# Batch 0's MLP over five feature steps on both token halves side by side, with a new order of mixing, weight steps and the second batch's scans

## The chip, the cores and the metric

The kernel runs on one core of a Trainium2 chip. The metric is the device time of one execution in microseconds (us). Engines are named as in the profile: PE (TensorE), DVE (VectorE), ACT (ScalarE), POOL (GpSimd) and SP (SyncE, which only issues transfers here).

## What is computed

Three stages follow each other for 4 batches of 768 tokens. A gated linear attention with 8 heads of width 48, whose outputs side by side are a row x of 384:

```
state = alpha[:, :, t, :, None] * state + einsum('bhd,bhe->bhde', k[:, :, t], v[:, :, t])
y[:, :, t] = einsum('bhd,bhde->bhe', q[:, :, t], state)
```

Then a mixer over tokens of rank 32 and an MLP over channels with 1536 features, and last a gating stage:

```
h = x.transpose(0, 2, 1) @ U @ V
u = x + h.transpose(0, 2, 1)
x2 = u + maximum(u @ w_ch1, 0.0) @ w_ch2

h = maximum(x2 @ w_in, 0.0)
u, v = h[..., :512], h[..., 512:]
v_n = (v - mean(v)) / sqrt(var(v) + 1e-06)
out = (u * (einsum('ts,bsd->btd', w_spatial, v_n) + b_spatial[None, :, None])) @ w_out
```

The weights of mixer, MLP and gating arrive as 64-bit words and are turned into float32 on the chip.

## The kernel before

The 768 tokens of a batch are two halves ("blocks") of 384, kept channels first: a block is a tile of 128 partitions x 3 feature tiles m x 384 tokens. Every large product is taken as three matmuls, of the high and low parts of its factors (`mm3`, L238 to L243).

**Scan.** The 8 heads of a batch make four pairs. `prepare` (L606) makes the running products of alpha with two scans on DVE (bw, L613; fw, L625) and scales k and q by them on POOL (L603). A `Pair` then has its transpositions on PE (`flip`, L654, tile ps_kt, copied by ACT to kn), two groups of scores (L669, ps_sc), masks on DVE (L678, sm), a state group (L694, ps_d) that DVE scans to after (L700) and ACT copies to state, and output groups (L716 inner, L725 outer, ps_y) that ACT copies (L738). `attend` (L800 on) yields between these as steps.

**Mixing.** `Mix` transposes a feature tile (L763, ps_t), ACT copies it (L770), PE multiplies by U (L779, ps_g), ACT and DVE make the stack stk (L786, L787), and `mix_sum` (L267 on) multiplies by V (ps_h), adds on DVE (L275), rounds to the high part on ACT (L276, partuh) and makes the remainder with `rest` (L207, partul) on DVE or POOL.

**Weights.** The 12 feature steps f of the MLP have one tile of weights each. A `Stage` brings one from DRAM and turns it: `begin` has ACT scale the low words (L195, bits), DVE do two operations (L196 and L199, narrow) and POOL one addition (L202); a first `finish` has ACT round to the high half (L505, w) and a second has DVE make the low half (L207, w).

**MLP.** `ChannelMlp.block` goes through feature steps for one block. `up_group` makes 9 matmuls into one of two banks "mm" (L321, tile ps); ACT makes h (L328) and DVE hl (`rest_of_h`, L309), both from the bank. Two groups later `down_group` makes 9 matmuls into three banks "acc" (L241 to L243, tile acc), and after the last feature step of a stretch DVE adds them to the block (L354). The third kind of banks, "x", also three, belongs to scan and mixing.

**Order.** PE has all engines' work in one hand-written order. Between groups of matmuls the MLP calls `pull` (L1018), which counts, begins and finishes weight steps at fixed remainders of the count, and runs steps of the next batch's scan so that they are spread over the count. For batch 0 the stretches of features are those of `FIRST`, each for block 0 and then block 1, and the first batch's own scan and mixing (`first_batch`, L889) stands ahead of the MLP or within its first groups. `busy` (L633) puts matmuls without use in PE's queue as fillers.

## Time and profile before

| | us |
|---|---|
| median of 3 runs (lowest to highest) | 723.58 (723.48 to 724.1) |
| span of the profiled execution, first to last instruction | 722.5 |
| PE busy | 699.7 (97%) |
| DVE busy | 341.0 (47%) |
| ACT busy | 267.1 (37%) |
| POOL busy | 203.8 (28%) |

The profiled execution's own time is not given beside its span; the median of the runs is 1.1 us above the span, and that is taken for what lies around it. Busy shares are means over the whole span. PE's idle time is nearly all in the first 92 us and in the last 8, so the first 92 us are read in windows. Each row of a timeline has its start, its length, engine, line, operation, output, inputs and shape; in brackets stands the engine's idle time before it and what ended it. Matmul lengths overlap: the pace is read from the difference of two starts.

### The profile page before, as it was taken

The page shows a single profiled execution, that of the slowest core. Times are in us where ns is not written, and L with a number is a line of the kernel's source. Part 1 is how long each engine was busy: PE and PEld are TensorE (multiplying, and loading weights), DVE is VectorE, ACT ScalarE, POOL GpSimd, SP SyncE. Part 2 cuts the span into 40 slices and gives each one's busy share as a digit, 9 for nine tenths or more (in the row PEclk, how much of TensorE's full clock was granted, in tenths as well). Part 3 has the DMA queues.
Part 4 walks back from the last instruction along what each step waited for, and adds up shares of the span by engine and source line. Part 5 has one row for each costly group of instructions (what it writes and reads, how often), then busy time and mean ns, then how long its engine had stood idle before and what let it go on. Part 6 is the DMA issues. An engine that isn't in the chain of part 4 may idle for free.

```text
span 722.5 us, 12138 instructions
## 1 busy us (share of the span) xinstructions
PE 699.7 (97%) x4984; PEld 665.8 (92%) x4984; DVE 341.0 (47%) x585; ACT 267.1 (37%) x542; POOL 203.8 (28%) x171
## 2 busy tenths in 40 slices
PE   7988699999999999999999999999999999999996
PEld 6877599999999999999999999989989989999996
DVE  8877879846444434443332486253152134226211
ACT  3874266643444332444331444232232223224111
POOL 4445434414110122010030043334224123433211
PEclk9999899999999999999999999999999999999998
DMA  9699043330532230500001545120003003000001
GB/s 343 205 341 222 1 80 70 67 68 34 109 73 48 61 59 1 111 5 2 34 1 37 189 131 169 48 73 1 34 1 99 33 1 99 1 33 2 33 34 38
DMA packets 21170, 54.01 MB, mean 75 GB/s; under 512 B 2705, under 2 KB 12817, under 8 KB 19825
## 3 DMA queue, kind: packets, MB, share of 16 engines
q1 hardware_dynamic: 21104, 53.14, 26.6%
q8 instruction: 41, 0.67, 0.4%
q14 instruction: 25, 0.20, 0.1%
HBM read 42.51 MB, written 9.44 MB: 72 GB/s over the span
## 4 chain that ended last, share of the span: by engine, by line
PE 86%; DVE 3%; ACT 1%; POOL 1%; issue 1%; POOLq 0%; ACTq 0%
PE ps L321 20%; PE acc L241 7%; PE acc L242 7%; PE acc L243 7%; PE ps_s L242 5%; PE ps_s L243 5%; PE ps_s L241 4%; PE ps_sc L669 3%; PE ps_y L716 2%; PE ps_o L243 2%; PE ps_o L242 2%; PE ps_o L241 2%; PE ps_v L242 2%; PE ps_v L241 2%; PE ps_v L243 2%; PE ps_u L242 2%
## 5 line engine op out<-in xcount | busy, mean ns | idle before, releaser
L321 PE MATMUL ps<-partuh,w 128*128 128x384 f32 x576 | 135.0, 341 | 7.5 <-ACT w L505 3.3
L321 PEld LDWEIGHTS ps<-partuh,w 128*128 128x128 f32 x576 | 102.8, 190 | 10.7 <-DVE w L207 4.0
L309 DVE SCALAR_TENSOR_TENSOR hl<-ps,h 128x384 fp32r<-128x384 f32 x96 | 53.1, 554 | 120.9 <-ACT h L328 120.1
L241 PE MATMUL acc<-h,w 128*128 128x384 f32 x288 | 99.5, 345 | 0.3 <-DVE ub L354 0.3
L243 PE MATMUL acc<-hl,w 128*128 128x384 f32 x288 | 96.7, 336 | 0.0
L242 PE MATMUL acc<-h,w 128*128 128x384 f32 x288 | 96.6, 335 | 0.0
L328 ACT ACTIVATE h<-ps 128x384 fp32r<-128x384 f32 x96 | 46.9, 488 | 97.3 <-PE ps L321 97.0
L454 DVE TENSOR_TENSOR vsb<-ps_s,bb 128x384 f32<-128x384 f32 x32 | 17.8, 558 | 127.3 <-PE ps_s L243 127.3
L207 POOL TENSOR_TENSOR partul<-ub,partuh 128x384 fp32r<-128x384 f32 x47 | 47.2, 1027 | 102.0 <-ACT partuh L276 89.1
L321 PE MATMUL ps<-partul,w 128*128 128x384 f32 x288 | 68.3, 344 | 1.1 <-POOL partul L207 1.0
L207 POOL TENSOR_TENSOR gl<-gt,gh 128x384 fp32r<-128x384 f32 x32 | 32.4, 1012 | 118.5 <-ACT gh L460 118.5
L242 PE MATMUL ps_s<-wsph,vl 128*128 128x384 f32 x192 | 64.5, 336 | 0.9 <-POOL vl L207 0.9
L241 PE MATMUL ps_s<-wsph,vh 128*128 128x384 f32 x192 | 64.2, 334 | 0.0
L243 PE MATMUL ps_s<-wspl,vh 128*128 128x384 f32 x192 | 64.2, 334 | 0.0
L460 ACT ACTIVATE gh<-gt 128x384 fp32r<-128x384 f32 x32 | 16.8, 526 | 124.5 <-DVE gt L457 124.5
L241 PEld LDWEIGHTS acc<-h,w 128*128 128x128 f32 x288 | 54.3, 189 | 2.9 <-issue 1.2
L242 PEld LDWEIGHTS acc<-h,w 128*128 128x128 f32 x288 | 54.3, 189 | 0.0
L321 PEld LDWEIGHTS ps<-partul,w 128*128 128x128 f32 x288 | 51.5, 191 | 3.0 <-POOL partul L207 1.9
L243 PEld LDWEIGHTS acc<-hl,w 128*128 128x128 f32 x288 | 54.2, 188 | 0.0
L603 POOL TENSOR_TENSOR akq<-akq,bw 128x768 f32<-128x768 f32 (+1 forms) x15 | 24.6, 1638 | 87.8 <-DVE bw L613 85.9
L207 POOL TENSOR_TENSOR vl<-vt,vh 128x512 fp32r<-128x512 f32 x20 | 27.2, 1383 | 50.0 <-ACT vh L424 50.0
L202 POOL TENSOR_TENSOR narrow<-narrow,bits 128x768 uint32<-128x768 uint32 (+2 forms) x14 | 27.7, 1981 | 45.8 <-ACT bits L195 16.0
(154 smaller groups left out, 1369.8 us busy)
## 6 DMA issues: line engine op xcount, KB each, us to landing
akq<-in_akq SPq DMA_DIRECT2D x24, 433.3 KB, 7.2
bits<-in_w SPq DMA_DIRECT2D x12, 768.0 KB, 12.7
x2d<-ub SPq DMA_DIRECT2D x8, 576.0 KB, 3.4
ub<-x2d SPq DMA_DIRECT2D x8, 576.0 KB, 5.2
out_y<-ob SPq DMA_DIRECT2D x24, 192.0 KB, 1.9
v<-in_v SPq DMA_DIRECT2D x15, 288.0 KB, 7.6
words<-in_w_in SPq DMA_DIRECT2D x8, 384.0 KB, 3.3
words<-in_wsT SPq DMA_DIRECT2D x4, 576.0 KB, 6.7
```

The costliest lines, as they stand in the source:

```text
L202: nc.gpsimd.tensor_tensor(out=t, in0=t, in1=low, op=ALU.add)
L207: engine.tensor_tensor(out=out, in0=x, in1=hi.bitcast(F32), op=ALU.subtract)
L241: nc.tensor.matmul(out=ps, lhsT=wh, rhs=xh, start=first, stop=False)
L242: nc.tensor.matmul(out=ps, lhsT=wl, rhs=xh, start=False, stop=False)
L243: nc.tensor.matmul(out=ps, lhsT=wh, rhs=xl, start=False, stop=last)
L309: nc.vector.scalar_tensor_tensor(out=hl, in0=ps[:, 0:TB], scalar=0.0, in1=h.bitcast(F32), op0=ALU.max, op1=ALU.subtract)
L321: nc.tensor.matmul(out=ps[:, 0:TB], lhsT=wx[:, k * 128 : (k + 1) * 128], rhs=ux[:, k, :], start=i == 0, stop=i == len(parts) - 1)
L328: nc.scalar.activation(out=h, in_=ps[:, 0:TB], func=AF.Relu)
L454: nc.vector.tensor_tensor(out=vsb, in0=psv[:, 0:TB], in1=self.g["bb"][:, blk * TB : (blk + 1) * TB], op=ALU.add)
L460: nc.scalar.activation(out=hi, in_=gt, func=AF.Copy)
L603: engine.tensor_tensor(out=chunks(x)[:, c], in0=chunks(x)[:, c], in1=chunks(by)[:, c, 1:CW], op=ALU.mult)
L669: nc.tensor.matmul(out=pts[h][:, j * C : (j + 1) * C], lhsT=self.k[r, c * C : (c + 1) * C], rhs=self.q[r, c * C : (c + 1) * C], start=True ...
```

## The change

The first five feature steps of batch 0 are run for both blocks in turn at each step (`side_by_side`), with block 0 accumulating in the banks "acc" and block 1 in the banks "x"; for the first of these steps both up groups are made together (`up_both`), all products with the inputs' high parts first. The remaining features follow as before, in the stretches 5 to 7 and 8 to 11. All mixing sums of batch 0 stand ahead of the MLP, and their remainders are shared out over POOL and DVE. The scaling of low words is taken out of `narrowed` (`low_part`) and can be issued early (`scale`); the first two weights' narrow words lie in places that the inputs' parts take later. `pull` begins weight steps at counts listed by hand, and holds the second batch to five steps until the banks "x" are given back.

```diff
-FIRST = (0, 2, 5, 8, 12)
+FIRST = (0, 5, 8, 12)
 N_WARM = 12
-PACE = 10
+BEGINS = (1, 9, 17, 25, 34, 43, 54, 65, 76, 87)
+AHEAD, N_AHEAD, HELD = 20, 5, 62
+ENDS = tuple(x + y for x in BEGINS for y in (10, 12))
...
+    def low_part(words):
+        low = words.rearrange("p (n w) -> p n w", w=2)[:, :, 0]
+        nc.scalar.activation(out=low, in_=low, func=AF.Copy, scale=2.0**-29)
...
-        rest(lo[:, m, :], t[:, m, :], hi[:, m, :], engine)
+        if engine:
+            rest(lo[:, m, :], t[:, m, :], hi[:, m, :], engine)
...
+        def side_by_side(self, b, blocks, f0, f1, tags):
+            self.held = True
+            for f in range(f0, f1):
+                self.need(f + 1)
+                for blk, h in enumerate(self.up_both(blocks, f) if f == f0 else (None, None)):
+                    h = h or self.up_group(blocks[blk], f)
+                    self.behind.append((b, blk, blocks[blk], f, h, f == f0, f == f1 - 1, tags[blk]))
+                    self.flush(2)
...
+        def up_both(self, blocks, f):
...
+            for ends in (False, True):
+                for (t, uh, ul), ps in zip(blocks, both):
+                    parts = [(wh, ul, k) for k in range(KE)] if ends else [(wx, uh, k) for wx in (wh, wl) for k in range(KE)]
...
                 for m in range(KE):
-                    nc.vector.tensor_tensor(out=t[:, m, :], in0=self.acc[m][:, 0:TB], in1=t[:, m, :], op=ALU.add)
+                    nc.vector.tensor_tensor(out=t[:, m, :], in0=acc[m][:, 0:TB], in1=t[:, m, :], op=ALU.add)
+                if tag != "acc":
+                    self.held = False
...
+                if n == 2:
+                    weights.scale()
+                    weights.scale()
...
-                next(ahead)
+                if n < NP - 2:
+                    next(ahead)
...
-            pair.inner(1)
-            pair.outer(0)
-            pair.outer(1)
-            pair.take(0)
-            pair.take(1, nc.vector)
+            for x in range(NB):
+                pair.inner(x)
+            for x in range(NB):
+                pair.outer(x)
+            for x in range(NB):
+                pair.take(x, nc.vector)
...
-            busy(4, ps.tile([128, 512], F32, "ps_w", "acc"))
-            summed(0, 0, nc.gpsimd)
-            weights.begin()
-            gp = mixes[2].product()
-            summed(0, 1, nc.gpsimd)
-            mixes[2].keep(gp)
-            busy(10, ps.tile([128, 512], F32, "ps_w", "acc"))
-            summed(0, 2)
+            summed(0, 0)
+            summed(1, 0)
+            gp = mixes[2].product()
+            mixes[2].keep(gp)
+            for blk in range(NB):
+                summed(blk, 1)
+                summed(blk, 2)
+            busy(4, ps.tile([128, 512], F32, "ps_w", "mm"))
+            for m, blk, engine in (
+                (0, 0, nc.gpsimd), (0, 1, nc.gpsimd), (1, 0, nc.gpsimd), (2, 0, nc.vector), (1, 1, nc.vector), (2, 1, nc.vector)
+            ):
+                t, hi, lo = blocks[blk]
+                rest(lo[:, m, :], t[:, m, :], hi[:, m, :], engine)
...
-            if pulls % PACE == 1:
-                if b == 0 and pulls == 1:
-                    weights.finish(1)
+            if b == 0 and pulls in ENDS:
+                weights.finish(1)
+            if b == 0 and pulls in BEGINS:
                 weights.begin()
-            elif pulls % PACE in (PACE - 3, 0):
-                weights.finish(1)
-            while done * (groups - late) < (pulls - late) * n_steps:
+            while done < due():
                 done += 1
                 next(steps, None)
+
+        def due():
+            if b > 0:
+                return -(-pulls * n_steps // groups)
+            if mlp.held or pulls <= HELD:
+                return min(N_AHEAD, (pulls - AHEAD) // 4)
+            return N_AHEAD + -(-(pulls - HELD) * (n_steps - N_AHEAD) // (groups - HELD))
...
-                for f0, f1 in zip(FIRST[:-1], FIRST[1:]):
+                mlp.side_by_side(b, blocks, *FIRST[0:2], ("acc", "x"))
+                for f0, f1 in zip(FIRST[1:-1], FIRST[2:]):
                     for blk in range(NB):
                         mlp.block(b, blk, blocks[blk], f0, f1)
```

The order of instructions shows it at three places. The numbers behind ps, acc and w tell one tile from another; lines of the changed kernel are its own (L221 there is L207 of before, L210 and L213 are L196 and L199, L334 is L309, L404 is L354).

DVE at the beginning of the MLP, before: the low half of weight step 1, the narrowing of step 2, the first hl, the sums of block 1, the next hl.

```order
L207 TENSOR_TENSOR partul<-ub,partuh 128x384
L207 TENSOR_TENSOR w_700<-narrow,w_700 128x768
L196 TENSOR_SCALAR narrow<-bits 128x768
L199 SCALAR_TENSOR_TENSOR narrow<-bits,narrow 128x768
L309 SCALAR_TENSOR_TENSOR hl<-ps_702,h 128x384
L275 TENSOR_TENSOR ub<-ps_h,ub 128x384 x3
L309 SCALAR_TENSOR_TENSOR hl<-ps_745,h 128x384
L309 SCALAR_TENSOR_TENSOR hl<-ps_759,h 128x384
L207 TENSOR_TENSOR w_778<-narrow,w_778 128x768
```

The same place with the change:

```order
L289 TENSOR_TENSOR ub<-ps_h,ub 128x384 x4
L221 TENSOR_TENSOR partul<-ub,partuh 128x384 x3
L221 TENSOR_TENSOR w_699<-narrow,w_699 128x768
L210 TENSOR_SCALAR narrow<-bits 128x768
L213 SCALAR_TENSOR_TENSOR narrow<-bits,narrow 128x768
L334 SCALAR_TENSOR_TENSOR hl<-ps_702,h 128x384
L334 SCALAR_TENSOR_TENSOR hl<-ps_703,h 128x384
L334 SCALAR_TENSOR_TENSOR hl<-ps_744,h 128x384
```

The sums of both blocks moved ahead of the first hl; the low half of weight 1 and the narrowing of step 2 still stand between them and it.

PE where the next batch's first transposition group ps_kt stands, before: in the middle of a down group into the banks "acc".

```order
L241 MATMUL acc_846<-h,w_700 128x384
L242 MATMUL acc_846<-h,w_700 128x384
L243 MATMUL acc_846<-hl,w_700 128x384
L654 MATMUL ps_kt<-ident,akq_83 128x128 x5
L241 MATMUL acc_847<-h,w_700 128x384
L242 MATMUL acc_847<-h,w_700 128x384
L243 MATMUL acc_847<-hl,w_700 128x384
```

With the change it follows the last matmul that accumulates in the banks "x" (acc_790 to acc_792), and the scores ps_sc come six MLP matmuls later, where there were 18:

```order
L255 MATMUL acc_792<-h,w_870 128x384
L256 MATMUL acc_792<-h,w_870 128x384
L257 MATMUL acc_792<-hl,w_870 128x384
L706 MATMUL ps_kt<-ident,akq_83 128x128 x5
L346 MATMUL ps_1066<-partuh,w_991 128x384 x3
L346 MATMUL ps_1066<-partul,w_991 128x384 x3
L721 MATMUL ps_sc<-akq_83 128x128 x6
```

DVE behind that place with the change, from the sums of the "x" banks to the first masks sm:

```order
L334 SCALAR_TENSOR_TENSOR hl<-ps_1021,h 128x384
L404 TENSOR_TENSOR ub<-acc_790,ub 128x384
L404 TENSOR_TENSOR ub<-acc_791,ub 128x384
L404 TENSOR_TENSOR ub<-acc_792,ub 128x384
L665 SCALAR_TENSOR_TENSOR bw<-akq_84,ends 128x774
L668 RECIPROCAL starts<-bw 128x6
L210 TENSOR_SCALAR narrow<-bits 128x768
L213 SCALAR_TENSOR_TENSOR narrow<-bits,narrow 128x768
L221 TENSOR_TENSOR w_1057<-narrow,w_1057 128x768
L730 TENSOR_TENSOR sm<-ps_sc,causal 128x384 x2
```

In before, a scan, a low half and a narrowing stand between sums and first masks too; with the change the sums ahead of them are those whose banks the scan itself takes.

## Rows read from the trace of the kernel before

**Rows 1.** The page, the clock that was granted in 40 equal slices.

```profile
PEclk9999899999999999999999999999999999999998
```

**Rows 2.** Waits of PE from 0 to 140 us: total, times, longest.

```profile
PE ps L321 <- ACT w L505: 3.3, 1, 3.3
PE ps L321 <- DVE w L207: 3.2, 2, 1.8
```

**Rows 3.** Windows, PE: length, busy time (instructions), mean clock, DMA share, GB/s.

```profile
51.26:91.78 40.52, 31.61 (x176) 0.87 0.49 113
91.78:172.50 80.72, 80.72 (x695) 1.00 0.36 71
53.40:56.80 3.40, 3.40 (x14) 0.59 1.01 290
80.90:86.90 6.00, 4.59 (x21) 0.50 0.00 0
```

**Rows 4.** Timeline of PE, 39 to 173 us.

```profile
39.28 1.26 PE L725 MATMUL ps_y<-akqvuh,state 128*48 128x128 f32 x20
...
51.55 0.51 PE L321 MATMUL ps<-partuh,w 128*128 128x384 f32 x2
...
91.96 0.33 PE L241 MATMUL acc<-h,w 128*128 128x384 f32 x1
...
93.00 0.68 PE L321 MATMUL ps<-partuh,w 128*128 128x384 f32 x3
...
94.13 1.52 PE L716 MATMUL ps_y<-sm,v 128*48 128x128 f32 x24
...
99.41 0.71 PE L654 MATMUL ps_kt<-ident,akq 128*128 128x128 f32 x5
...
102.14 0.94 PE L669 MATMUL ps_sc<-akq 64*128 64x128 f32 x12
...
172.50 0.71 PE L654 MATMUL ps_kt<-ident,akq 128*128 128x128 f32 x5
```

**Rows 5.** Timeline of DVE and POOL, single rows from 42 to 125 us.

```profile
42.25 1.11 DVE L740 COPY ub<-ps_y 48x384 f32<-48x384 f32 x2
...
50.92 0.28 DVE L787 TENSOR_TENSOR stk<-ps_g,stk 32x128 fp32r<-32x128 f32 x1 [0.75 <-ACT stk L786]
...
85.69 1.84 POOL L202 TENSOR_TENSOR narrow<-narrow,bits 128x768 uint32<-128x768 uint32 x1 [3.64 <-ACT bits L195]
...
88.23 1.76 DVE L625 TENSOR_TENSOR_SCAN fw<-akq,starts 128x774 f32<-128x774 f32 x1
...
95.37 0.55 DVE L196 TENSOR_SCALAR narrow<-bits 128x768 uint32<-128x768 uint32 x1
...
123.68 1.68 POOL L603 TENSOR_TENSOR akq<-akq,bw 128x768 f32<-128x768 f32 x1
123.70 3.29 DVE L625 TENSOR_TENSOR_SCAN fw<-akq,starts 128x774 f32<-128x774 f32 x1
```

**Rows 6.** Groups by line, 92 to 160 us: count, busy us, mean ns, idle before.

```profile
L309 DVE SCALAR_TENSOR_TENSOR hl<-ps,h 128x384 fp32r<-128x384 f32 x13 | 7.1, 546 | 7.4 <-ACT h L328 7.2
L207 DVE TENSOR_TENSOR w<-narrow,w 128x768 fp32r<-128x768 f32 x7 | 6.9, 984 | 0.6 <-ACT w L505 0.6
L354 DVE TENSOR_TENSOR ub<-acc,ub 128x384 f32<-128x384 f32 x12 | 5.9, 546 | 0.0
L199 DVE SCALAR_TENSOR_TENSOR narrow<-bits,narrow 128x768 uint32<-128x768 uint32 x6 | 5.7, 958 | 0.2
...
L505 ACT ACTIVATE w<-narrow 128x768 fp32r<-128x768 f32 x7 | 5.9, 842 | 3.1 <-POOL narrow L202 3.1
L738 ACT ACTIVATE ub<-ps_y 48x384 f32<-48x384 f32 x12 | 5.8, 484 | 2.7 <-PE ps_y L725 2.6
...
L202 POOL TENSOR_TENSOR narrow<-narrow,bits 128x768 uint32<-128x768 uint32 x6 | 13.0, 2159 | 22.7 <-DVE narrow L199 9.7 <-ACT y L738 5.4 <-ACT bits L195 4.5
L603 POOL TENSOR_TENSOR akq<-akq,bw 128x768 f32<-128x768 f32 x3 | 5.1, 1696 | 4.3 <-DVE bw L613 4.3
```

More of the change, by code (lines that the diff above doesn't have):

```diff
@@ L163, in begin @@
                 return False
-            while len(self.late) > 1:
+            while len(self.late) > self.most:
                 self.finish()
@@ L167, in begin @@
             if wide and not place:
-                t = self.narrow()[0 : words.shape[0], 0:n]
+                t = (room or self.narrow())[0 : words.shape[0], 0:n]
+            if wide and not self.scaled:
+                low_part(words)
+            self.scaled = max(0, self.scaled - 1)
             x = narrowed(words, t) if wide else words
@@ L194, in narrowed @@
         low, high = words[:, :, 0], words[:, :, 1]
-        nc.scalar.activation(out=low, in_=low, func=AF.Copy, scale=2.0**-29)
         nc.vector.tensor_scalar(
@@ L300, in block @@
                     self.rest_of_h()
-                self.behind.append((b, blk, block, f, h, f == f0, f == f1 - 1))
+                self.behind.append((b, blk, block, f, h, f == f0, f == f1 - 1, "acc"))
                 self.flush(2)
@@ L330, in up_group @@
             return h, hl
+        def up_both(self, blocks, f):
+            w = self.wts
+            wh, wl = w[f][:, 0], w[f][:, 1]
+            both = [self.psp.tile([128, 512], F32, name="ps_1", tag="mm") for _ in blocks]
+            for ends in (False, True):
+                for (t, uh, ul), ps in zip(blocks, both):
+                    parts = [(wh, ul, k) for k in range(KE)] if ends else [(wx, uh, k) for wx in (wh, wl) for k in range(KE)]
+                    for i, (wx, ux, k) in enumerate(parts):
+                        nc.tensor.matmul(
+                            out=ps[:, 0:TB], lhsT=wx[:, k * 128 : (k + 1) * 128], rhs=ux[:, k, :],
+                            start=i == 0 and not ends, stop=ends and i == KE - 1,
+                        )
+                    self.pull()
+            hs = []
+            for ps in both:
+                h = self.hp.tile([128, TB], F32R, name="h", tag="h", bufs=3)
+                hl = self.hp.tile([128, TB], F32R, name="hl", tag="hl", bufs=3)
+                nc.scalar.activation(out=h, in_=ps[:, 0:TB], func=AF.Relu)
+                self.h = ps, h, hl
+                self.rest_of_h()
+                hs.append((h, hl))
+            return hs
         def flush(self, most=0):
@@ L337, in flush, with down_group @@
                 self.down_group(*self.behind.pop(0))
-        def down_group(self, b, blk, block, f, h, begin, end):
+        def down_group(self, b, blk, block, f, h, begin, end, tag):
             t = block[0]
@@ L342, in down_group @@
             if begin:
-                self.acc = [self.psp.tile([128, 512], F32, name=f"acc{m}", tag="acc") for m in range(KE)]
+                self.accs[blk] = [self.psp.tile([128, 512], F32, name=f"acc{m}", tag=tag) for m in range(KE)]
+            acc = self.accs[blk]
             for m in range(KE):
@@ L347, in down_group @@
                 o = slice(E + m * 128, E + (m + 1) * 128)
-                mm3(self.acc[m][:, 0:TB], (w[f][:, 0, o], w[f][:, 1, o]), h, begin, end)
+                mm3(acc[m][:, 0:TB], (w[f][:, 0, o], w[f][:, 1, o]), h, begin, end)
                 if m < KE - 1 - end:
@@ L878, in gla_mixer_gating_kernel @@
         homes = lambda: w12s.raw(NF1 - 2), lambda: w12s.raw(NF1 - 1)
[L879 removed]
+        weights = Stage(apool, [*small_items(g, homes), *w12s.items()], width=2 * E, most=2)
         N_SMALL = 2
@@ L941, in first_batch @@
                 pair = after
-            weights.begin()
+            narrow = [up.pool.tile([128, KE * TB], U32, name="narrow", tag=x) for x in ("uh0", "ul0")]
+            weights.begin(narrow[0])
+            weights.begin(narrow[1])
+            weights.scale()
             before()
@@ L947, in first_batch @@
             later = pair.scores(1)
+            weights.begin()
             pair.state(pd)
+            pair.mask(later)
             for m in range(KE):
@@ L951, in first_batch @@
             flipped(0)
-            pair.inner(0)
-            pair.mask(later)
+            weights.finish(1)
             weights.begin()
+            for x in range(NB):
[4 more added lines that the diff above has]
+                pair.take(x, nc.vector)
             weights.finish(1)
             flipped(1)
-            weights.begin()
-            pair.inner(1)
-            pair.outer(0)
-            pair.outer(1)
-            pair.take(0)
-            pair.take(1, nc.vector)
+            weights.finish(1)
+            weights.finish(1)
             gp = mixes[0].product()
```

32 lines of the change are left out of this document (15 added, 17 removed).

## The prediction

> **What bounds the kernel now.** I read the page first: TensorE (PE) is the engine that sets the time, and its granted clock is below full level in few places [rows 1]. So the time can fall only where PE idles or runs at the low clock. The waits of PE up to 140 us show who holds it up: the weights of batch 0's MLP, twice through VectorE (DVE) and once through ScalarE (ACT), together 6.5 us [rows 2]. The windows place it: from 51.26 to 91.78 us PE is busy 31.61 of 40.52 us at a mean clock of 0.87, and from 91.78 to 172.50 it is never idle and always at full clock [rows 3]. The low level (1.2 GHz) is granted for some 3.4 us from 53.4, after two idle gaps, and for some 6 us from 80.9, after PE had waited for weights [rows 3]; everywhere else in the stretch it is 2.4 GHz. Whatever this change gives or takes must come from there.
>
> **A common mark.** I count only matmuls of the MLP (up and down). From the 417th on, where a transposition group of the third batch's scan is next, PE's two orders read alike to the end of the program. Before reaches that mark at 172.50 us [rows 4] and PE is full from there. So the difference of the two times is the difference at this mark.
>
> **Work without waits.** Six MLP matmuls took 1.04 us (91.96 to 93.00), 0.173 us each [rows 4]. The first group of the second batch's scores-times-values (94.13) stands behind 132 MLP matmuls: 132 x 0.173 = 22.9 us, and the first pair's transpositions, two score groups and state group before it are about 0.7 + 0.9 + 0.9 = 2.5 us [rows 4] and, for the state group, a like 0.8. From 94.13 to the mark PE is full: 78.4 us. Together 104.6 us. Before began this work at 51.55 [rows 4] and took 120.95 us for it, with three mixing sums (0.75) in between: 15.6 us are lost to idle time and clock. That is what there is to win; the rest is when the changed kernel can begin, and what new waits it makes.
>
> **The beginning.** The change takes the mixing of all three feature tiles and all six sums ahead of the MLP, has DVE do all four copies of the last pair's output, moves the low parts of u and v earlier and the last alpha pass out of the stretch, and leaves 14 of the 18 filler matmuls out. The last outer products run from 39.28 for 1.26 us in before [rows 4]; without the transposition that stood in between and its wait for ACT I put their end at 39.2. Then in series: four copies on DVE, 2.2 us (two took 1.11 [rows 5]), 41.4; transposition, copies on ACT, product of the third tile and its two copies. In before this took from 43.36 to the stack's last copy, 50.92 + 0.28 [rows 5], 7.8 us, with fillers and two sums in between; without them I take 5.3, so 46.7, and keep 7.8 for the range. Then four sums on DVE at 0.55 [rows 6], three remainders at about 0.5 (half the columns of a low half) and the low half of weight step 1 (0.98 [rows 6]), to 51.2. Meanwhile PE does the first feature step of both halves, the low parts of the inputs last, and ends it at 51.1 with 18 MLP matmuls done. Its next group reuses the first group's bank, which is free only when DVE has made hl from it; and ahead of that hl DVE has the two narrowing operations of weight step 2 (0.55 [rows 5] and 0.96 [rows 6]). So hl ends at 53.2 and PE idles 2.1 us. The sum starts there: at 53.2, with 104.6 - 18 x 0.173 = 101.5 us to go, the mark would be reached at **154.7** without another wait.
>
> **DVE and GpSimd (POOL) share something.** A scan of 128x774 takes 1.76 us alone; at 123.70 it took 3.29, and POOL's product had started at 123.68 and lasted 1.68: it ended 1.63 us before the scan did [rows 5]. The narrowing takes 0.55 us alone [rows 5], while POOL's addition takes 1.84 alone [rows 5] and 2.16 in the mean [rows 6]. DVE's operations with an input in PSUM (hl, sums) keep their 0.55 us [rows 6] beside POOL. So an operation of DVE between SBUF tiles and one of POOL run one after the other. I carried this through the new order of DVE, instruction by instruction, with these durations.
>
> **New waits.** Per feature step (two up groups and two down groups, 36 x 0.173 = 6.2 us of PE) DVE has one weight step (0.55 + 0.96 + 0.98) and two hl (1.1): 3.6 us, and POOL 1.84. That fits, where before read a weight every 3.1 us within a block and waited. But between feature steps 2 and 4 the next batch's first scans come in, 3.5 us on DVE and 3.4 on POOL (two products of 1.70 [rows 6]), one after the other. A hl is then late, and since only two banks take the up groups, PE waits for it: 0.8, 1.4 and 1.0 us at three up groups, **3.3** with a rest of 0.1. When the six banks are given back, the scan's transposition follows at once on the bank of the second half's first tile, whose sum stands on DVE behind three sums of the first half and a hl: **1.9**. Then the second scan (1.76), a narrowing behind POOL's product, and a low half stand ahead of the first masks, and the second group of scores needs the bank that they read: **2.6**. The scan that follows delays the next masks, and the output group waits: **1.4**. After that DVE catches up; two or three waits of 0.3 to 1.5 remain by my reckoning, but I had taken PE's output groups some 0.6 us too short each, which takes most of them away: **0.8**. Sum 10.0 us.
>
> **Clock.** I expect one fall after the 2.1 us of idle time, as in before after about as much. 3.4 us at half speed cost 1.7 us [rows 3]; but the waits of 3.3 us behind it come from DVE being late against PE, and shrink by as much when PE is later. I set it at nothing; if the cover is gone it costs 1.7.
>
> **What else moves.** All weights are issued by SyncE in the same order as before, and are in SBUF well before their use: nothing. The second batch's loads stand in the same order in SyncE's queue: nothing, covered by the slack of the scans. Three blocks of features instead of four save six sums of 0.55 us on DVE [rows 6], 3.3 us, which is in the reckoning. The steps of the second batch are held to five until the banks are free and then go 39 in 74 pulls, against 44 in 117: this density is what the waits above price; below it is nothing, as the full stretch after 91.78 shows, where DVE was as busy without a wait of PE; above it is the second rival.
>
> **The sum.** 154.7 + 10.0 = 164.7 at the mark, against 172.50: 7.8 us less. The span of 722.5 becomes 714.7. The median of the runs, 723.58, is 1.1 above the span, so the forecast is **715.8 us**.
>
> **Rivals.**
> 1. *DVE's lag never reaches PE.* For it: from 91.78 to 172.50 PE did not wait at all [rows 3] although DVE did scans and weights there as well. Against it: the new order has the scans nearer together, and waits for banks. Then the mark is at 154.7 and the time 705.8. Chance 0.2.
> 2. *DVE and POOL wholly in series*, with nothing of POOL beside DVE's operations on PSUM. From 51.2 to the last mask of the fourth pair DVE has, by [rows 5, 6], ten narrowings (15.1), ten low halves (9.8), 17 hl (9.3), 12 sums (6.6), five pairs of scans (18.6) and masks, states and stacks (7.5): 67 us; POOL has ten additions (18.4) and ten products (17.0): 35.4. In series they end at 153.6, against 144.3 in my reckoning: 9.3 us more, 725.1. Against it: the PSUM operations at 0.55 us. Chance 0.1. The Trainium skill, "SBUF — State Buffer", section "SBUF: two separate sides", has the pair's lock held for a whole instruction, with the other engine fully blocked; by that rule a collision costs the whole of the other's operation, as the 3.29 us scan shows, and this rival is the case in which every pair collides.
> 3. *DVE stands behind ACT.* The low half of a weight on DVE waits for ACT's high half; where that stands behind four output copies it comes 4 x 0.484 + 0.842 = 2.8 us late [rows 6], and every hl, mask and sum behind it on DVE waits too. My sum has this once, hidden. From three more of the ten weight steps on (7.8 / 2.8) nothing is won, and with six more the time is 715.8 + 16.8 = 732.6: slower. Against it: before, DVE idled only 0.6 us for this in seven weight steps [rows 6]; for it: the copies now come nearer together. Chance 0.08.
> 4. *The change doesn't do what it says*: some weight is still late at its step, or a load is, and PE waits for it as before, twice 3.3 us [rows 2] on top: 722.4. Chance 0.04.
> 5. *The clock falls again and again*: at each of the five further waits of 1 us and more as it did at 53.4, 5 x 1.7 = 8.5 us more, 724.3. Against it: in before the two falls stand behind about 2 and 5 us of idle time, and the new waits are mostly shorter. Chance 0.05. The Trainium skill, "TensorE: Matmul & The Clock Gate", section "A second HAM failure mode: psum-queue depth-cycling", tells of a kernel that cycles through PSUM banks and whose PE idles briefly between matmul groups, often enough that the clock goes to and fro; by that rule a change that makes PE wait for banks pays more than its waits, and no stretch of this trace shows it.
>
> **How the numbers follow.** The forecast has 0.53 (709 to 721: waits from 3 to 15 us), the rivals 0.2, 0.1, 0.08, 0.04 and 0.05. A measurement of this kernel can tell 0.2%, 1.4 us: faster is below 722.1, slower above 725.0. Faster: 0.53 + 0.2, a third of the second rival's and half of the fourth's and fifth's, 0.8. Same: the rest of those three but 0.03, 0.09. Slower: the third and those 0.03 of the second, 0.11. The range reaches from 706 (no new wait) to 722.5 (the fourth rival).
>
> **What would show it.** In the changed profile: the first up group's end near 51 us and a gap of about 2 us before the next, released by DVE's hl; no PE wait for a weight; the gaps at the bank hand-over and at the first two score and output groups, released by DVE's sum and masks, near 88, 94 and 100 us; the transposition of the mark near 165 us. It is wrong if PE waits for ACT or for weights, or if the mark comes later than 172 us.

## The result and the profile after

| | before | after |
|---|---|---|
| median of 4 runs (lowest to highest), us | 723.53 (723.01 to 724.1) | 717.43 (716.6 to 717.8) |
| span of the profiled execution, us | 722.5 | 715.8 |
| start of the transposition of the common mark, us | 172.50 | 166.55 |

The ratio is 0.991, with a 95% interval of 0.9898 to 0.9922: 6.1 us less, where 7.8 were forecast. The mark comes 5.95 us earlier and the span is 6.7 us shorter, so nearly all of the gain lies ahead of the mark.

The page's clock row, for [rows 1], has nothing below 9 any more:

```profile
PEclk9999999999999999999999999999999999999999
```

The waits of PE from 0 to 140 us, for [rows 2]. No wait for a weight is left; the largest are DVE's hl, its masks, and a transposition:

```profile
PE ps L346 <- DVE hl L334: 4.2, 4, 1.5
PE ps_sc L721 <- DVE sm L730: 1.7, 1, 1.7
PE ps_kt L706 <- issue: 1.5, 1, 1.5
```

The windows, for [rows 3] (length, busy time, mean clock). Where before lost 8.9 us to idle time in 40.5 us at a clock of 0.87, after loses 4.2 in 33.7 at full clock; but the part up to the mark, which was full before, now has another 4.2 us of idle time, and 3.4 us at the lower clock:

```profile
51.26:85.00 33.74, 29.51 (x166) 1.00 0.59 137
85.00:166.55 81.55, 77.32 (x690) 0.98 0.35 70
97.95:101.35 3.40, 3.40 (x16) 0.50 0.00 0
```

The timeline of PE, for [rows 4]: the start of the MLP, and every group that waited for 0.6 us or more up to 100 us (in brackets the idle time and what ended it):

```profile
48.95 2.35 PE L366 MATMUL ps<-partuh,w 128*128 128x384 f32 x12
51.15 1.21 PE L366 MATMUL ps<-partul,w 128*128 128x384 f32 x6
53.90 0.79 PE L346 MATMUL ps<-partuh,w 128*128 128x384 f32 x3 [1.54 <-DVE hl L334]
...
70.64 0.79 PE L346 MATMUL ps<-partuh,w 128*128 128x384 f32 x3 [0.87 <-DVE hl L334]
...
75.21 0.81 PE L346 MATMUL ps<-partuh,w 128*128 128x384 f32 x3 [1.17 <-DVE hl L334]
...
79.28 0.80 PE L346 MATMUL ps<-partuh,w 128*128 128x384 f32 x3 [0.65 <-DVE hl L334]
...
90.48 0.86 PE L706 MATMUL ps_kt<-ident,akq 128*128 128x128 f32 x5 [1.53 <-issue]
...
97.56 2.11 PE L721 MATMUL ps_sc<-akq 64*128 64x128 f32 x12 [1.70 <-DVE sm L730]
...
166.55 0.71 PE L706 MATMUL ps_kt<-ident,akq 128*128 128x128 f32 x5
```

DVE's timeline says what stands behind these waits, for [rows 5]: at 53.3 the hl behind a low half and a narrowing, at 67 a narrowing beside POOL's product, and at 91 to 97 everything that is ahead of the first masks:

```profile
50.97 0.94 DVE L221 TENSOR_TENSOR w<-narrow,w 128x768 fp32r<-128x768 f32 x1
51.84 0.55 DVE L210 TENSOR_SCALAR narrow<-bits 128x768 uint32<-128x768 uint32 x1
52.42 0.96 DVE L213 SCALAR_TENSOR_TENSOR narrow<-bits,narrow 128x768 uint32<-128x768 uint32 x1
53.29 1.01 DVE L334 SCALAR_TENSOR_TENSOR hl<-ps,h 128x384 fp32r<-128x384 f32 x2
...
67.08 2.05 DVE L210 TENSOR_SCALAR narrow<-bits 128x768 uint32<-128x768 uint32 x1
...
89.84 1.47 DVE L404 TENSOR_TENSOR ub<-acc,ub 128x384 f32<-128x384 f32 x3
91.23 1.76 DVE L665 TENSOR_TENSOR_SCAN bw<-akq,ends 128x774 f32<-128x774 f32 x1
93.02 0.19 DVE L668 RECIPROCAL starts<-bw 128x6 f32<-128x6 f32 x1
93.13 2.05 DVE L210 TENSOR_SCALAR narrow<-bits 128x768 uint32<-128x768 uint32 x1
95.22 0.96 DVE L213 SCALAR_TENSOR_TENSOR narrow<-bits,narrow 128x768 uint32<-128x768 uint32 x1
96.09 0.95 DVE L221 TENSOR_TENSOR w<-narrow,w 128x768 fp32r<-128x768 f32 x1
96.96 1.01 DVE L730 TENSOR_TENSOR sm<-ps_sc,causal 128x384 f32<-128x384 f32 x2
```

The transposition at 90.48 is put down to "issue", but DVE's three sums of the banks "x" begin at 89.84 and end at 91.3, overlapping, and the first of them, at 0.55 us as in [rows 6], is done at 90.4: PE went on 0.1 us later. That it had waited for this sum is read from the times alone. POOL's products at the two narrowings of 2.05 us are these:

```profile
67.01 1.70 POOL L655 TENSOR_TENSOR akq<-akq,bw 128x768 f32<-128x768 f32 x1 [2.58 <-DVE bw L665]
...
93.06 1.70 POOL L655 TENSOR_TENSOR akq<-akq,bw 128x768 f32<-128x768 f32 x1 [3.75 <-DVE bw L665]
```

### The profile page after: what moved, and what is told of

The parts are those of the page before. It is cut to its first block, busy times and chain, and to the rows that moved or that the text cites. A ratio compares the mean times of both kernels' runs of the same rounds, so it can differ in the third digit from the quotient of the medians.

```text
span 715.8 us, 12096 instructions
## 1 busy us (share of the span) xinstructions
PE 695.0 (97%) x4956; PEld 661.3 (92%) x4956; DVE 343.7 (48%) x583; ACT 265.3 (37%) x540; POOL 201.0 (28%) x169
## 4 chain that ended last, share of the span: by engine, by line
PE 81%; DVE 11%; ACT 3%; issue 2%; DMA 1%; POOL 0%; SPq 0%; DVEq 0%; ACTq 0%
PE ps L346 18%; PE acc L255 6%; PE acc L257 6%; PE acc L256 6%; PE ps_s L256 5%; PE ps_s L257 5%; PE ps_s L255 5%; PE ps_sc L721 3%; PE ps_o L257 2%; PE ps_o L256 2%; PE ps_o L255 2%; PE ps_y L768 2%; PE ps_v L256 2%; PE ps_v L255 2%; PE ps_v L257 2%; DVE bw L665 2%
## 5 line engine op out<-in xcount | busy, mean ns | idle before, releaser
L346 PE MATMUL ps<-partuh,w 128*128 128x384 f32 x564 | 130.5, 339 | 4.2 <-DVE hl L334 4.2
L334 DVE SCALAR_TENSOR_TENSOR hl<-ps,h 128x384 fp32r<-128x384 f32 x96 | 53.0, 553 | 112.9 <-ACT h L353 112.3
L346 PEld LDWEIGHTS ps<-partuh,w 128*128 128x128 f32 x564 | 100.0, 189 | 6.3 <-DVE hl L334 5.5
L255 PE MATMUL acc<-h,w 128*128 128x384 f32 x288 | 99.3, 345 | 0.3 <-DVE ub L404 0.3
L256 PE MATMUL acc<-h,w 128*128 128x384 f32 x288 | 96.5, 335 | 0.0
L221 POOL TENSOR_TENSOR partul<-ub,partuh 128x384 fp32r<-128x384 f32 x45 | 46.0, 1046 | 98.5 <-ACT partuh L290 85.7
L221 POOL TENSOR_TENSOR gl<-gt,gh 128x384 fp32r<-128x384 f32 x32 | 32.5, 1014 | 118.5 <-ACT gh L512 118.5
L346 PE MATMUL ps<-partul,w 128*128 128x384 f32 x282 | 65.5, 340 | 0.0
L256 PE MATMUL ps_s<-wsph,vl 128*128 128x384 f32 x192 | 64.5, 336 | 0.9 <-POOL vl L221 0.9
L255 PE MATMUL ps_s<-wsph,vh 128*128 128x384 f32 x192 | 64.2, 335 | 0.0
L255 PEld LDWEIGHTS acc<-h,w 128*128 128x128 f32 x288 | 54.2, 188 | 3.0 <-issue 1.3
L256 PEld LDWEIGHTS acc<-h,w 128*128 128x128 f32 x288 | 54.3, 189 | 0.0
L346 PEld LDWEIGHTS ps<-partul,w 128*128 128x128 f32 x282 | 49.6, 188 | 1.5 <-issue 0.7
L221 POOL TENSOR_TENSOR vl<-vt,vh 128x512 fp32r<-128x512 f32 x20 | 27.2, 1382 | 50.0 <-ACT vh L476 50.0
L655 POOL TENSOR_TENSOR akq<-akq,fw 128x768 f32<-128x768 f32 (+1 forms) x15 | 24.9, 1658 | 46.4 <-DVE fw L677 41.5
```

What stands on the lines that cost most here:

```text
L221: engine.tensor_tensor(out=out, in0=x, in1=hi.bitcast(F32), op=ALU.subtract)
L255: nc.tensor.matmul(out=ps, lhsT=wh, rhs=xh, start=first, stop=False)
L256: nc.tensor.matmul(out=ps, lhsT=wl, rhs=xh, start=False, stop=False)
L334: nc.vector.scalar_tensor_tensor(out=hl, in0=ps[:, 0:TB], scalar=0.0, in1=h.bitcast(F32), op0=ALU.max, op1=ALU.subtract)
L346: nc.tensor.matmul(out=ps[:, 0:TB], lhsT=wx[:, k * 128 : (k + 1) * 128], rhs=ux[:, k, :], start=i == 0, stop=i == len(parts) - 1)
L655: engine.tensor_tensor(out=chunks(x)[:, c], in0=chunks(x)[:, c], in1=chunks(by)[:, c, 1:CW], op=ALU.mult)
```

## The experiments

Each is measured against the kernel before on its own chip, which took 724.35, 724.48, 724.03 and 724.57 us there. By its ratio of 0.991 the changed kernel stands at 717.8 to 718.0 in these series; in the third it was run again.

### Is the first stage's new order needed?

The old end of the first batch (fillers, order of the mixing sums, POOL for the remainders, copies shared with ACT) with the rest of the change as it is:

```diff
-            for blk in range(NB):
-                summed(blk, 1)
-                summed(blk, 2)
-            busy(4, ps.tile([128, 512], F32, "ps_w", "mm"))
...
+            busy(10, ps.tile([128, 512], F32, "ps_w", "acc"))
+            summed(0, 2)
...
+            for m in range(KE):
+                summed(1, m, nc.gpsimd)
```

> The end of the first batch (last pair, transpositions, products, sums, fillers, weight steps 0 and 1) is that of the kernel before, with block 1's three sums put ahead of the MLP because both halves are wanted at once; the rest is the changed kernel. Theory: the MLP's first matmul comes at some 52 us in place of 49 and its second group at 56 to 57 in place of 53.9, so 720 to 722.5. Rival (the start doesn't matter, since DVE's lag later sets PE): 717 to 718.5.

Measured: 723.31 us in the median of ten runs, ratio 0.9982 (0.9969 to 0.9995): 5.4 us worse than the changed kernel, a little more than expected. The ten runs lie far apart, from 721.96 to 726.2 us; the four quickest (up to 722.36) are 4.0 to 4.4 us worse, and the trace is that of the longest. PE's timeline in it shows that the later start is carried on:

```profile
54.30 1.89 PE L366 MATMUL ps<-partuh,w 128*128 128x384 f32 x6 [0.91 <-ACT partuh L290]
...
59.61 0.96 PE L346 MATMUL ps<-partuh,w 128*128 128x384 f32 x3 [0.84 <-DVE hl L334]
...
97.32 0.86 PE L706 MATMUL ps_kt<-ident,akq 128*128 128x128 f32 x5 [1.51 <-issue]
```

The second round of up groups begins 5.71 us later (59.61 against 53.90), the bank hand-over 6.84. Little of it is taken back: the first two waits for hl are 0.84 and 0.34 us, where the changed kernel has 1.54 and 0.87, and the others stay as they were. But the clock adds to it in this trace: it is 0.50 from 60.05 to 63.45 us, where the changed kernel has no fall, and from 104.45 to 111.25, twice as long as the changed kernel's. So the start is worth 4 to 5.4 us, of which a part comes by way of the clock.

### Is running side by side needed?

The first five steps block by block, in the stretches of before, with all else as in the change:

```diff
-FIRST = (0, 5, 8, 12)
+FIRST = (0, 2, 5, 8, 12)
...
-                mlp.side_by_side(b, blocks, *FIRST[0:2], ("acc", "x"))
-                for f0, f1 in zip(FIRST[1:-1], FIRST[2:]):
+                pass
+                for f0, f1 in zip(FIRST[:-1], FIRST[1:]):
```

> The first five feature steps are done block by block in the stretches 0 to 1 and 2 to 4, in the three banks acc, as before the change; mixing, weight steps and pace of the scans stay the changed kernel's. Theory (PE waits where DVE is late; the order of weight steps gives most of the gain): the weights 2, 3 and 4 are ready at 59, 65 and 73 us and would be wanted at some 66, 69 and 73, so waits for weights of 0 to 3 us come back, the wait of 1.5 us at the hand-over of six banks goes, and six sums of 0.55 us come to DVE: 716 to 720. Rival (doing the halves side by side is what wins, by halving the rate of weights): the waits of the kernel before come back, 6 us and more, 722 or above.

Measured: 727.92 us, ratio 1.0047 (1.0031 to 1.0063): slower than the kernel before. My theory fell. The waits for weights are back, through DVE and through ACT, and so is a low clock (0.63 from 70 to 74 us, 0.52 from 74 to 78):

```profile
66.21 0.79 PE L346 MATMUL ps<-partuh,w 128*128 128x384 f32 x3 [1.17 <-DVE w L221]
...
70.56 0.94 PE L346 MATMUL ps<-partuh,w 128*128 128x384 f32 x3 [1.99 <-ACT w L557]
...
73.96 1.33 PE L346 MATMUL ps<-partuh,w 128*128 128x384 f32 x3 [1.50 <-DVE w L221]
...
103.50 1.40 PE L721 MATMUL ps_sc<-akq 64*128 64x128 f32 x12 [3.23 <-DVE sm L730]
```

An earlier start alone is not kept, since the weights are not ready earlier. With two blocks on one weight PE needs a weight every 6.2 us instead of every 3.1. The lists of pulls stayed those made for two blocks at a step; block by block with lists of its own was not tried.

### Four steps side by side, and the old pace of weights

```diff
-FIRST = (0, 5, 8, 12)
+FIRST = (0, 4, 8, 12)
...
-AHEAD, N_AHEAD, HELD = 20, 5, 62
+AHEAD, N_AHEAD, HELD = 20, 5, 50
```

> Four feature steps side by side in place of five, the next stretch 4 to 7; the scans are let go at pull 50 and not 62, so 39 steps go over 86 pulls in place of 74. Theory (DVE's lag is set by its work and POOL's, which only moves): weights 5 to 7 are wanted earlier, at a rate of one every 3.1 us, and waits for them of up to 3 us appear, while the waits at the hand-over and at the first scores get smaller: 716 to 720. Rival (the density of the scans sets the waits): 712 to 715.5.

Measured: 720.66 us, ratio 0.9947 (0.9931 to 0.9964). The hand-over comes earlier and DVE is not: the transposition at 86.05 waits 3.11 us, the output group at 116.00 waits 3.21 for the state scan, and behind each the clock is 0.50 for 3.4 us. There is no wait for a weight, and the wait at the hand-over is longer instead of shorter: the theory's mechanism was wrong.

Weight steps begun and ended every ten pulls, as before:

```diff
-            if b == 0 and pulls in ENDS:
-                weights.finish(1)
-            if b == 0 and pulls in BEGINS:
+            if b == 0 and pulls % 10 == 1:
+                if pulls == 1:
+                    weights.finish(1)
                 weights.begin()
+            elif b == 0 and pulls % 10 in (7, 0):
+                weights.finish(1)
```

> Weight steps of batch 0 begin and end at the fixed remainders of the kernel before (begun at every tenth pull, ended at 7 and 10), in place of the lists. Theory: with the halves side by side a weight is wanted every 12 pulls, and one every 10 is early enough: 716 to 719. Rival (the hand-made lists are a part of the gain): 720 or above.

Measured: 719.47 us, ratio 0.9938 (0.9921 to 0.9954), 1.5 us worse, which is hardly clear of the noise. The wait at the hand-over is 3.46 us (92.87) instead of 1.53, and one hl wait is 1.91 (75.09). Both times were a little above what I expected: the lists and the five steps are each a small part of the gain. This trace too has two falls of the clock (0.50 from 75.35 to 78.75 and from 92.40 to 95.80), the changed kernel's has one; how much of either loss is the waits and how much the clock was not separated.

### What makes DVE late: POOL's addition?

Three kernels change only POOL's addition of the low bits, for weight steps 2 to 11. In the first DVE joins the words, in the second nothing does, in the third POOL adds as before, but into a tile that nobody reads:

```diff
-        nc.gpsimd.tensor_tensor(out=t, in0=t, in1=low, op=ALU.add)
+        adder.tensor_tensor(out=t, in0=t, in1=low, op=ALU.add if adder is nc.gpsimd else ALU.bitwise_or)
```

> The last of three operations of weight steps 2 to 11 (joining low and high words, 1.84 us on POOL) is done by DVE instead, as a bitwise or of 0.96 us; a carry out of the low word is lost there. Theory (DVE's operations between SBUF tiles and POOL's run one after the other): DVE gets some 9 us of work more, but is rid of the stretches in which it stood behind POOL's addition (6.9 us up to 100 us in the changed kernel's trace): 715.5 to 719.5, and no narrowing or low half of more than 1.0 us but beside the scan's products. Rival (POOL's addition lies beside DVE's work, and DVE's own busy time is what makes it late): 8 us of work more before the hand-over of the banks, 722 to 727.

```diff
-        nc.gpsimd.tensor_tensor(out=t, in0=t, in1=low, op=ALU.add)
+        if not bare:
+            nc.gpsimd.tensor_tensor(out=t, in0=t, in1=low, op=ALU.add)
```

> Weight steps 2 to 11 leave out joining the low words (POOL's addition), so their weights lack the last three bits. Theory: DVE is not held behind POOL's addition any more (6.9 us up to 100 us), of which about 4 reach PE: 712 to 714.5, with narrowings and low halves at 0.55 and 0.96 us but beside the scan's products. Rival (DVE's own work, the hand-over of banks and the density of the scans make the waits): 716.5 or above, with PE's waits for hl, sums and masks as they are.

```diff
-        nc.gpsimd.tensor_tensor(out=t, in0=t, in1=low, op=ALU.add)
+        if aside:
+            nc.gpsimd.tensor_tensor(out=beside[0], in0=t, in1=ends[:, 0 : 2 * E].bitcast(U32), op=ALU.add)
+        else:
+            nc.gpsimd.tensor_tensor(out=t, in0=t, in1=low, op=ALU.add)
```

> As the run without POOL's addition, but POOL makes an addition of the same size into a tile that nobody reads, at the same place in its order, so that POOL is as busy as in the changed kernel while no weight waits for it (the weights lack the low words' three bits). Theory (DVE's operations between SBUF tiles stand behind POOL's): the longer narrowings and low halves of DVE come back, and the time is 715.5 to 718.5 against 712.9 without the addition. Rival (the gain of that run was the shorter chain of a weight, since ACT's high half did not wait for POOL any more): 712 to 714.

Measured: joined by DVE 720.54 us, ratio 0.9954 (0.9937 to 0.997); left out 712.89, ratio 0.9844 (0.9827 to 0.986); made aside 716.25, ratio 0.9889 (0.9873 to 0.9906). Joined by DVE the time is above the theory's range and below the rival's; the other two are as the theory had them. Left out, the addition saves 4.9 us. Made aside, with nobody waiting for it, it gives back 3.4 of these: that is the price of POOL being occupied. The other 1.5 to 1.7 would be the chain through it, but the intervals of this ratio and the changed kernel's overlap, so that part is not shown. In the two traces (711.96 and 716.34 us) the hand-over's transposition comes at 86.66 without the addition and at 90.28 with it aside, 3.6 us later by waits of PE; a fall of the clock (0.50 from 99.00 to 102.40), which only the second has, adds 1.5. The groups of DVE by line, 52 to 110 us (count, busy us, mean ns, idle before), first of the changed kernel:

```profile
L221 DVE TENSOR_TENSOR w<-narrow,w 128x768 fp32r<-128x768 f32 x8 | 11.8, 1475 | 2.0 <-ACT w L557 2.0
L210 DVE TENSOR_SCALAR narrow<-bits 128x768 uint32<-128x768 uint32 x9 | 11.3, 1257 | 0.0
...
L334 DVE SCALAR_TENSOR_TENSOR hl<-ps,h 128x384 fp32r<-128x384 f32 x14 | 7.6, 547 | 4.4 <-ACT h L353 4.4
L665 DVE TENSOR_TENSOR_SCAN bw<-akq,ends 128x774 f32<-128x774 f32 x3 | 7.0, 2331 | 0.0
```

Without the addition (its L222 is L221 here):

```profile
L210 DVE TENSOR_SCALAR narrow<-bits 128x768 uint32<-128x768 uint32 x9 | 9.2, 1026 | 0.0
...
L222 DVE TENSOR_TENSOR w<-narrow,w 128x768 fp32r<-128x768 f32 x9 | 8.6, 952 | 1.2 <-ACT w L558 1.2
...
L666 DVE TENSOR_TENSOR_SCAN bw<-akq,ends 128x774 f32<-128x774 f32 x3 | 5.3, 1763 | 0.0
```

With the addition made aside (L226 is the low half, L212 the narrowing):

```profile
L226 DVE TENSOR_TENSOR w<-narrow,w 128x768 fp32r<-128x768 f32 x9 | 12.4, 1378 | 2.1 <-ACT w L562 2.1
L212 DVE TENSOR_SCALAR narrow<-bits 128x768 uint32<-128x768 uint32 x9 | 11.3, 1251 | 0.0
```

A low half takes 0.95 us when POOL adds nothing and 1.38 to 1.48 when it does, whoever reads the sum; hl, which has an operand in PSUM, keeps 0.55. The narrowing of 67.08 ends 0.42 us after POOL's product of 67.01 does, as if it had waited for all of it. So the two engines do exclude each other, in these instructions between SBUF tiles. By the Trainium skill, "SBUF — State Buffer", section "SBUF: two separate sides", whichever of the two starts first gets the shared pair of ports for its whole instruction; these rows agree. Moving the work from POOL to DVE does not pay here: joined by DVE, the low halves are back at 0.95 us, but each weight step has 0.96 us more on DVE, the first gap grows from 1.54 to 2.62 us and the masks' wait from 1.70 to 2.74.

### Can a wait be taken away, or does it only move?

Weight step 2 begun four pulls later, so that the first hl do not stand behind its narrowing:

```diff
-BEGINS = (1, 9, 17, 25, 34, 43, 54, 65, 76, 87)
+BEGINS = (5, 9, 17, 25, 34, 43, 54, 65, 76, 87)
...
-ENDS = tuple(x + y for x in BEGINS for y in (10, 12))
+ENDS = (11, 13) + tuple(x + y for x in BEGINS[1:] for y in (10, 12))
```

> Weight step 2 begins at pull 5 and not at pull 1, so that DVE makes the first two hl before its narrowing; its two later parts stay at pulls 11 and 13. Theory (the gap of 1.5 us before the second group of up matmuls is DVE's narrowing ahead of hl): the gap is under 0.4 us and the time 715.4 to 716.7. Rival (the lag only moves on: weight 2 or a later hl is late by as much): 717 to 718.

Measured: 718.51 us, ratio 0.9919 (0.99 to 0.9939), no gain, and above both ranges. The first gap shrinks by 0.89 us and the next wait grows by 1.02 (0.87 before); the clock fell behind it too (0.50 from 71.90 to 75.30):

```profile
53.15 0.79 PE L346 MATMUL ps<-partuh,w 128*128 128x384 f32 x3 [0.65 <-DVE hl L334]
...
70.91 0.81 PE L346 MATMUL ps<-partuh,w 128*128 128x384 f32 x3 [1.89 <-DVE hl L334]
```

Then the changed kernel again as it is, and with weight steps later (9 to 11 begun later, the two halves of 8 to 11 made later), so that the narrowing and the low half of 93.13 to 97.04 stand behind the masks:

```diff
-BEGINS = (1, 9, 17, 25, 34, 43, 54, 65, 76, 87)
+BEGINS = (1, 9, 17, 25, 34, 43, 54, 72, 82, 90)
...
-ENDS = tuple(x + y for x in BEGINS for y in (10, 12))
+ENDS = (11, 13, 19, 21, 27, 29, 35, 37, 44, 46, 53, 55, 70, 72, 82, 84, 92, 94, 100, 102)
```

> The changed kernel itself, on the same chip as the two above, as the mark they are measured from: 717 to 718.5 by both.

> The changed kernel with weight steps 8 to 11 begun later (at pulls 72, 82 and 90 instead of 65, 76 and 87, and their ends moved with them), so that the second pair of scans and the first masks stand ahead of the narrowing and the low half that stood between them. Theory (the lag of DVE against PE is what is lost, and at the first masks it is worth the narrowing and the low half ahead of them, 2.05 + 0.87 us): the 1.7 us wait for the masks goes, and with it the fall of the clock behind it (1.7 us): 714.5 to 717 on a chip where the kernel before takes 724. Rival (the lag only moves on, to a later mask, output group or weight): a wait of 1 us or more comes behind the scores, or PE waits for a weight again: 717 to 719.5.

and with step 2 and the first scans spread as well:

```diff
-BEGINS = (1, 9, 17, 25, 34, 43, 54, 72, 82, 90)
-AHEAD, N_AHEAD, HELD = 20, 5, 62
+BEGINS = (5, 9, 17, 25, 34, 43, 54, 72, 82, 90)
+AHEAD, N_AHEAD, HELD = 12, 5, 62
```

> The kernel with later weight steps 8 to 11, and in addition weight step 2 begun at pull 5 instead of 1 and the second batch's first five steps from pull 12 instead of 20, so that no two of DVE's loads of this stretch come together. Theory (lag is made where scans and weight steps come together, so spreading them takes part of the 4.2 us of waits for hl as well): 713.5 to 716. Rival (DVE's and POOL's work up to the bank hand-over is the same in sum, so the lag there is the same whatever the order): as the kernel with later weight steps alone, within 1 us, the waits for hl standing at other steps with 3.5 to 4.5 us in sum.

Measured, on one chip: the changed kernel 717.81 us, ratio 0.9908 (0.9894 to 0.9922); weight steps later **714.44**, ratio 0.9866 (0.9851 to 0.9882), which beats both kernels; spread as well 715.71, ratio 0.9882 (0.9866 to 0.9897). The later weight steps in the trace:

```profile
90.58 0.86 PE L706 MATMUL ps_kt<-ident,akq 128*128 128x128 f32 x5 [1.55 <-issue]
...
115.43 1.66 PE L768 MATMUL ps_y<-sm,v 128*48 128x128 f32 x23 [1.61 <-DVE after L752]
...
163.23 0.71 PE L706 MATMUL ps_kt<-ident,akq 128*128 128x128 f32 x5
```

Its masks start at 93.41 instead of 96.96, and the scores no longer wait. A wait of 1.61 us comes 18 us later, so the lag does move on, as the rival had it; what does not come back is the fall of the clock. From 85 us to the mark:

```profile
85.00:163.23 78.23, 74.93 (x692) 1.00 0.38 73
```

against 81.55, 77.32 in the changed kernel: 0.93 us less idle time, and 2.39 us less busy time for the same work, with the clock at 2.4 GHz throughout. How much of this is the clock, the same 24 matmuls tell in three kernels, from the second scores to the next down group. In the changed kernel, from 97.56 on, with the wait and the fall:

```profile
102.59 0.33 PE L255 MATMUL acc<-h,w 128*128 128x384 f32 x1
```

Without POOL's addition, with the same wait and no fall (clock 1.00; its L722 and L256 are L721 and L255 here):

```profile
93.74 1.40 PE L722 MATMUL ps_sc<-akq 64*128 64x128 f32 x12 [1.68 <-DVE sm L731]
...
97.26 0.33 PE L256 MATMUL acc<-h,w 128*128 128x384 f32 x1
```

With weight steps later, with neither:

```profile
95.94 0.94 PE L721 MATMUL ps_sc<-akq 64*128 64x128 f32 x12
...
99.00 0.33 PE L255 MATMUL acc<-h,w 128*128 128x384 f32 x1
```

They take 5.03, 3.52 and 3.06 us. So the fall costs 1.5 us, and matmuls right behind a wait, slower even at full clock, another 0.46; the rest of the 2.39 is spread over the stretch in small pieces. The fall that did not come is 1.5 of the 3.4 us gained, the rest is waits and what follows them.

With the scans spread as well, the hand-over no longer waits, but one hl waits 2.59 us at 73.84 (clock 0.57 from 74 to 78 us) and a weight 1.03: DVE's work up to 90 us is the same, only its place differs. The time lies in the range of the theory, but it is 1.3 us above that with later weight steps alone, and the waits for hl, 3.95 us in sum, speak for the rival.

Last, the low half that stood ahead of the 1.61 us wait put behind the masks, too:

```diff
-ENDS = (11, 13, 19, 21, 27, 29, 35, 37, 44, 46, 53, 55, 70, 72, 82, 84, 92, 94, 100, 102)
+ENDS = (11, 13, 19, 21, 27, 29, 35, 37, 44, 46, 53, 55, 70, 72, 82, 86, 92, 94, 100, 102)
```

> The kernel with later weight steps 8 to 11, and in addition the low half of weight step 9 taken at pull 86 instead of 84, so that on DVE it stands behind the state scan and the masks of the second batch's second pair instead of ahead of them. In the kernel with later weight steps this low half took 2.55 us beside a POOL addition, and PE waited 1.61 us for that state scan. Theory (a wait goes where the work ahead of its releaser can be put behind it, because DVE then idles before the next stretch): the wait goes and no other of over 0.5 us comes in its place: 1.0 to 1.6 us below the kernel with later weight steps, 712.5 to 714 where the kernel before takes 724. Rival (the lag moves on to the next reader of DVE's work, the sums or the low half itself): 714 to 715, with a wait of 1 us or more between 116 and 130 us.

Measured: 714.43 us, ratio 0.9861 (0.9845 to 0.9878), the same as without. The wait of 1.61 us is gone, and two come in its place, of 0.54 and 0.71 us:

```profile
125.68 0.79 PE L746 MATMUL ps_d<-v,kn 128*64 128x48 f32 x20 [0.54 <-DVE sm L730]
...
130.47 1.55 PE L831 MATMUL ps_g<-yb,u 128*96 128x128 f32 x12 [0.71 <-DVE after L752]
```

The theory was wrong: the wait moved on to the next readers, as the rival had it, though in two pieces. This wait had no fall of the clock behind it, and moving it gained nothing.

## Why the prediction was right

The direction, the mechanism and the size held: 717.43 us measured, 715.8 forecast.

- *The beginning.* First groups done at 51.1 by the forecast, at 52.4 in the trace (51.15 + 1.21); next up group at 53.2 by the forecast, at 53.90 in the trace, 1.54 us of idle time instead of 2.1, released by the hl behind the narrowing as predicted. The forecast's own terms from 46.7 on add up to 51.4, not to the 51.2 that it has. The start is a real part of the gain: undone, it costs 5.4 us in the median and 4.0 in the quickest run.
- *Weights.* No PE wait for a weight is left, where before had 6.5 us; the fourth rival is out. Running block by block brings them back.
- *hl.* Three waits at the steps predicted, 0.87, 1.17 and 0.65 us where 0.8, 1.4 and 1.0 were forecast.
- *Hand-over.* 1.53 us, forecast 1.9. *Scores.* 1.70, forecast 2.6. *Output group.* 1.4 forecast, none recorded at 103.21: the term was too large. *Rest.* 0.8 forecast; 0.30 at 113.73 and 0.63 at 133.94.
- *Waits in sum.* 10.0 us forecast from 53.2 on; the windows have 4.23 + 4.23 - 1.54 = 6.9. The mark came 1.9 us later than forecast all the same, for the other terms.
- *Clock.* This is the step that was mis-sized. I had one fall after the first gap and set it at nothing, because shorter waits behind it would pay for it. The first gap brought none; one came behind the scores' wait, from 97.95 to 101.35, with only 0.30 and 0.63 us of recorded waits between it and the mark that it could have shrunk. Held against the same matmuls at full clock, it costs 1.5 us. "If the cover is gone it costs 1.7" was the right clause. The forecast also read the falls of before a little off: the trace of before has the clock at 0.50 from 52.80 to 56.15 and from 80.10 to 86.85, so the second is 6.8 us long and not 6.
- *Work without waits.* 101.5 us of work were reckoned from the start to the mark. The kernel with later weight steps, without a fall, takes 109.20 us (54.03 to 163.23) with 4.25 - 1.57 + 3.30 = 6.0 idle, so the work is 103.2: the term was 1.7 us short; why was not traced. In the changed kernel PE is busy 105.7 us over the same work; 1.5 of the 2.5 between them is the fall, the other 1.0 slower matmuls behind the masks' wait and small pieces.
- Start 0.7 late, work 1.7, clock 1.5 and those pieces 1.0 too small, waits 3.1 too large: 1.8 us in sum, of the 1.85 that separate 166.55 from 164.7. The forecast was nearer than its terms because their errors had opposite signs: that much of it is luck.
- *Rivals.* "DVE's lag never reaches PE" is out by 6.9 us of waits. "Wholly in series" is out by hl at 547 ns beside POOL, though the exclusion itself is worth some 3.4 us, part of it through the clock. DVE behind ACT came once, 1.84 us at 108.20 and hidden, as the sum had it. The clock fell once, not at five waits. That fifth rival stood beside a rule of the Trainium skill, "TensorE: Matmul & The Clock Gate", section "A second HAM failure mode: psum-queue depth-cycling"; six waits for banks with one fall show no such to and fro here.

The parts do not add up: undoing the start costs 5.4 us, side by side 10.1, the lists of pulls 1.5, together 17 where the whole change gains 6.1. Side by side without the new start is 0.2% below the kernel before, the new start without side by side is above it: neither gains much without the other, and the earlier start is only kept because two blocks share a weight.

What stays open: which part of the gain the fillers left out have (not tried alone), why the clock fell behind some waits and not behind others, and how often it does: each kernel left one trace, and the changed one two, with the fall behind the same wait.

## What to carry to other kernels

If PE waits for something that is made once per step, let two independent blocks use it in turn: the maker then has twice the time, and undoing it here cost 10 us. When an engine off the critical path is late, reordering its work mostly moves the wait to its next reader (three experiments); fewer collisions with POOL took the lag away (4.9 us), and more work on DVE in their place brought it back. Among waits of like length, look first for the one behind which the clock falls: moving that one paid 3.4 us, moving another of about the same length nothing.

## What the runs showed of the hardware

- The clock did not follow the length of the wait before it alone. Of the eleven waits of PE of 1.89 to 3.46 us between 45 and 200 us in all these traces, ten had a fall about their end, and one, of 2.62 us at 55.16 (words joined by DVE), had none. Waits of 1.54 to 1.61 us were followed by no fall in any of these traces. Waits of 1.67 to 1.70 us for the masks were followed by one in five traces (the changed kernel twice, weight step 2 later, addition aside, old start); but a like wait of 1.68 us was not where POOL's addition was left out, nor was one of 1.79 us at 73.35 in the kernel before. With the old start, three waits of 0.83 to 0.91 us from 54.3 to 59.6 were followed by a fall at 60.05.
- A fall of 3.4 us cost 1.5 us against the same 24 matmuls behind the same wait at full clock (5.03 and 3.52 us), close to the 1.7 that half speed over that length gives. The same matmuls took 3.06 us where no wait stood ahead of them, so 0.46 us of a wait's cost shows as busy time.
- A scan of 1.76 us took 3.48 at 109.07 in the changed kernel, beside an addition of POOL's that began at 109.05; the other two bw of that stretch took 1.76, and in the aside kernel, with POOL's additions at other places, all three did. Whether a scan is hit depends on where the addition falls, not on its being there.
